# A linear-attention and gated-MLP mixer on one core: the query features of the first row pair are turned early and stored turned

## The chip, the cores and the metric

One core of one Trainium2 chip runs the kernel. The metric is the device time of one execution in microseconds (us); of several runs the median is given. The engines are TensorE (PE), VectorE (DVE), ScalarE (ACT), GpSimd (POOL) and SyncE (SP); SP and POOL also issue DMA transfers.

## What is computed

x has 2048 rows of 512 values, in float32. After a layernorm two branches are added to it:

```python
xn = layernorm(x)
q, k, v = heads(xn @ wqkv)                 # 32 heads of 16
phi(t) = [softmax(t @ w_phi), softmax(-t @ w_phi)]     # 32 features a head
o = phi(q) (phi(k)^T v) / (phi(q) . sum(phi(k)) + 1e-6)
z = gelu(xn @ w_in); z1, z2 = z[:, :688], layernorm(z[:, 688:])
g = w_sp @ z2 + b_sp                       # w_sp is 2048 x 2048
out = x + o @ wo + (z1 * g) @ w_out
```

## The kernel before

The rows are 16 tiles of 128 (NT), or 8 pairs (NP). Every large product is made of three TensorE passes over float32 operands that are split in a high and a low half: L56 high by high, L57 high by low, L58 low by high (function mm3). ScalarE rounds the high half (L48, names in h), VectorE subtracts to get the low one (L52, names in l).

The stages follow one another, and TensorE has work in each:

- *Projections.* q, k, v and z1. The features of q, unnormalised, go to DRAM (e_d, one 128x1088 block a tile, with the inverse sums), z1 to z_d.
- *The z1 tail* (L631 to L647): the last z1 rows; zb, the sum of phi(k) over all rows, and kvT; then for the tiles s = 0 and 1 the features are loaded back (load_q) and normalised on VectorE (q_fin, L542 to L549: a multiplication with zb, a reduction, small steps, a reciprocal, a multiplication). The finished tile is stored to e_d by SP (L647). That store, `early`, is what the 15 copies of x into out (`seeds`, L708) are issued after, and behind them on SP stand 11 loads of w_sp (wf, L568).
- *The z2 stage* (L704 on): z2 of all tiles, gelu on ScalarE, layernorm statistics on VectorE (BN_STATS, L719), and b_split, which writes the B operands of the next stage.
- *The g stage* (products n = 0 to NC-1): w_sp times z2 by a seven-product scheme, four quarters a pair of row tiles; `drain` collects the products in c (L771 to L776), `gate` multiplies with z1, and `turn` transposes the gated pair in blocks of 32x32 on VectorE (L795, z1t<-c) and stores it to u_d with four DMAs (L798), for pair NP-2 = 6 through POOL and for the others through SP. In its last quarters the loads of the last stage are started too: zb, u of tiles 0 and 1, and with first_q the normalised features of tiles 0 and 1 (eq<-e_d, L835).
- *The last stage* (L993 on). For each pair of tiles: `attend_T` turns the features on TensorE (16 transposes, ptq, L934/L936) and ScalarE copies the four results to SBUF (f, L938); `project_u` is the product with w_out (pout, 15 matmuls by mm3 and two of L965), whose operands uh and ul are split from u; `attend` is the product with kvT (po, L951) and its split in oT high (ACT) and oT low (DVE); `project_o` adds oT times wo into pout; ScalarE copies pout and POOL adds it into out (L983, L984). Before the first pair the wo loads (16 DMAs, L808) are issued and split in woh and wol. Between the pairs VectorE normalises the features of the tiles three ahead (`features`), and POOL copies them (er<-et, L905) to the buffer that the transposes read.

Which instruction follows which on an engine is set by the Tile scheduler when the program is built, from its own estimate of the times; `tc.issue_after` lays down that an instruction may not be placed before another one. Each engine then works its list in order, and an instruction that waits holds up all behind it. Buffers come from pools; a tile placed where an earlier tile was waits for the last use of that one, a DMA's end too. The stage pool of the attention (cwk) lies where the buffers of the g stage were.

Of the kernel before, what the change touches and what calls it, by code (L numbers as in the profile page):

```python
# [10 lines left out]
F32 = mybir.dt.float32  # L11
F32R = mybir.dt.float32r
# [6 lines left out]
P = 128  # L19
# [4 lines left out]
NG = 4  # L24
NF = 2 * D
# [3 lines left out]
BL = 32  # L29
# [4 lines left out]
NP = NT // 2  # L34
# [6 lines left out]
def mixer(ctx: ExitStack, tc: tile.TileContext, x, x_t, wv, wqkT, phi_bd, wo, w_in, wst, b_r, w_out, out):  # L41
    nc = tc.nc
    pe, act, dve, pool, sp = nc.tensor, nc.scalar, nc.vector, nc.gpsimd, nc.sync
# [20 lines left out]
    left = lambda name, bufs: pool_of(name, bufs, side="left")  # L64
# [10 lines left out]
    dram = ctx.enter_context(tc.tile_pool(name="dram", bufs=1, space=DRAM))  # L75
    e_d = dram.tile([NT, P, NF + 2 * H], F32, name="e_d")
    z1_d = dram.tile([NT, P, FH], F32, name="z1_d")
    u_d = dram.tile([NT, FU, P], F32, name="u_d")
    kvT_d = dram.tile([P, D], F32, name="kvT_d")
    zb_d = dram.tile([P, NF], F32, name="zb_d")  # L80
    nm_d = dram.tile([NT, ND, P], F32, name="nm_d")

    ident = cst.tile([P, P], F32, name="ident")
# [16 lines left out]
    def group(e, j):  # L100

        return e[:, j * P:(j + 1) * P]
# [72 lines left out]
    with ExitStack() as p0:  # L175
# [236 lines left out]
        t = xz_tile(2 * D, F32R, "xT").rearrange("p (a b) -> p a b", a=2)  # L412
# [18 lines left out]
        p = ps.tile([P, D], F32, tag="mm", name="proj")  # L431
# [7 lines left out]
        p = ps.tile([P, D], F32, tag="mm", name="proj")  # L439
# [18 lines left out]
        p = ps.tile([P, D], F32, tag="mm", name="proj")  # L458
# [79 lines left out]
    def q_fin(et, tmp, zb):  # L538

        e, r, t, w = et[:, :NF], *(et[:, NF + k * 2 * H:NF + (k + 1) * 2 * H] for k in range(3))  # L540
        den = et[:, NF + 6 * H:QW]
        dve.tensor_tensor(tmp, e, zb, op=ALU.mult)  # L542
        dve.tensor_reduce(t, heads(tmp), axis=AX.X, op=ALU.add)
        dve.tensor_tensor(t, t, r, op=ALU.mult)
        dve.scalar_tensor_tensor(den, pairs(t, 0), EPS_DEN, pairs(t, 1), op0=ALU.add, op1=ALU.add)
        dve.reciprocal(den, den)
        dve.tensor_tensor(w.rearrange("p (h a) -> p h a", a=2), r.rearrange("p (h a) -> p h a", a=2),
                          den.unsqueeze(2).to_broadcast([P, H, 2]), op=ALU.mult)
        return e, dve.tensor_tensor(heads(e), heads(e), bc(w, 2 * H), op=ALU.mult).ins  # L549

    QC = 4
    NQ = NT // QC
    NC = NP * NQ
# [43 lines left out]
    NE = 2  # L597
    with ExitStack() as p1:
        tmp1 = p1.enter_context(left("tmp1", 1))
        kvT = tmp1.tile([P, D], F32, name="kvT")  # L600
        zb = tmp1.tile([P, NF], F32, name="zb")
        zhl = tmp1.tile([P, 4, D], F32R, tag="zhl", name="zhl")
        psk = p1.enter_context(psum("psk", 2))

        def make_zb():

            ones_r = tmp1.tile([P, P], F32R, name="ones_r")
            round_h(act, ones_r, ones)
            for k in range(2):
                pz = psk.tile([P, D], F32, tag="kvt", name="pz")  # L610
                cs = slice(k * D, (k + 1) * D)
                h, l = (zhl[:, 2 * k + n] for n in range(2))
                round_h(act, h, zacc[:, cs])
                rest_l(l, zacc[:, cs], h)
                pe.matmul(pz, ones_r, h, start=True, stop=False)
                pe.matmul(pz, ones_r, l, start=False, stop=True)
                dve.tensor_copy(zb[:, cs], pz)

        def make_kvT():
            kvm = zw.tile([P, 4, FC], F32, tag="T", name="kvm").rearrange("p a b -> p (a b)")[:, :D]  # L620
            kvm = kvm.rearrange("p (g b) -> p g b", b=P)
            dve.tensor_tensor(kvm.rearrange("p g (k b) -> p g k b", k=2),
                              kv_acc.unsqueeze(2).to_broadcast([P, NG, 2, HP]),
                              mask.rearrange("p (k b) -> p k b", k=2).unsqueeze(1).to_broadcast([P, NG, 2, HP]),
                              op=ALU.mult)
            pt = psk.tile([P, NG, P], F32, tag="kvt", name="kvt")
            for g in range(NG):
                pe.transpose(pt[:, g], kvm[:, g], ident)
            act.activation(kvT, pt.rearrange("p g b -> p (g b)"), AF.Copy)

        for j in range(2):  # L631
            load_win(w2[j], 2 + j)
        for s in range(NT - LAG, NT):
            z1_raw(tmp1, (za, zbp)[s % 2], s, 2)
            if s == NT - LAG + 1:
                make_zb()
        make_kvT()
        raw[0], raw[1] = load_a(0), load_a(1)
        A[0] = prep_a(0, raw.pop(0))
        sp.dma_start(kvT_d, kvT)  # L640
        sp.dma_start(zb_d, zb)
        tb = p1.enter_context(left("tmp1b", 1))
        for s in range(NE):
            et = load_q(s, tb.tile([P, QW], F32, name="et") if s else tmp1.tile([P, 4, D], F32, tag="zhl", name="et").rearrange("p a b -> p (a b)")[:, :QW])
            tmp = zw.tile([P, 4, FC], F32, tag="z2", bufs=2, name="qtmp").rearrange("p a b -> p (a b)")[:, :NF]
            e, _ = q_fin(et, tmp, zb)
            early = sp.dma_start(e_d[s, :, :NF], e).ins  # L647
    ctx_w1.__exit__(None, None, None)
    ctx_zc = psum("zc", 1)
    zc = ctx_zc.__enter__()  # L650
# [53 lines left out]
    for s in range(NT):  # L704
        p = zproj((kv_ps_p, zc, zbp, za)[s % 4], s, w2, (0, 1) if s % 2 == 0 else (1, 0))
# [7 lines left out]
        for k, q in p:  # L713
            ins = act.activation(z[:, k], q, AF.Gelu_apprx_tanh, scale=r_x[:, s:s + 1]).ins
# [87 lines left out]
    def slot(name, dt=F32):  # L802
        return xz_tile(2 * FH, dt, name)
# [26 lines left out]

    lasts, wu = [None] * 9, []

    def first_q(s):
        e = slot("eq", F32R)[:, :NF]
        sp.dma_start(e.bitcast(F32), e_d[s, :, :NF])  # L835
        return e

    def stage_w():
        t = [xz2.tile([P, SL], F32, tag="b", name="wof") for _ in range(3)]
        w = [xz_tile(2 * D, F32R, "wu") for _ in range(KF + 1)]  # L840
# [7 lines left out]
    g, es, ets = {}, {}, {}  # L848
    for n in range(NC):
        i = SEQ[n][0]  # L850
        if n % NQ == 1 and i < NP - 1:
            z = load_z1(i)
        products(n, g)
        if n % NQ == NQ - 1 and i < NP - 1:
            c = gt.tile([P, 2, FU], F32, tag="c", name="c")
            cq = c[:, :, :FH].rearrange("p k (j f) -> p k j f", j=2)
            cb = drain(i, g, cq)
            g = {}
        if n + 3 < NC:
            raw[n + 3] = load_a(n + 3)  # L860
        if n + 2 < NC:
            A[n + 2] = prep_a(n + 2, raw.pop(n + 2))
        if n % NQ == NQ - 1 and i < NP - 1:
            turn = gate(i, cb, z, c, z, prep_a.last)
            if i < NP - 2:
                turn()
        if n == NC - 4:
            stage_w()
        if n == NC - 3:
            zs = slot("zb", F32R)  # L870
            zb, ident_r = zs[:, :NF].bitcast(F32), zs[:, NF:NF + P]
            round_h(act, ident_r, ident)
            sp.dma_start(zb, zb_d)
            uT = [first_gate(0)]
            ets[2] = load_q(2, slot("et"))
            es[2], last = q_fin(ets.pop(2), slot("qtmp")[:, :NF], zb)
        if n == NC - 2:
            es[0], es[1] = first_q(0), first_q(1)
            t = xz_tile((KF + 1) * P, F32R, "u1")
            us = {1: load_u(1, k_tiles(t[:, :KF * P]).bitcast(F32), t[:2 * REM, KF * P:(KF + 1) * P])}  # L880
    cb = drain(NP - 1, g, slot("c").rearrange("p (k j f) -> p k j f", k=2, j=2))
# [9 lines left out]
    fin = []  # L891
# [33 lines left out]
    def attend_T(s):  # L925

        fs = []
        for g in range(NG):
            pt = pst.tile([P, 2, 2, P], F32, tag="tr", name="ptq")
            for a in range(2):  # L930
                for k in range(2):
                    src = group(es[s + k], 2 * g + a)
                    if src.dtype == F32:
                        pe.transpose(pt[:, a, k], src, ident)  # L934
                    else:
                        pe.transpose(pt[:, a, k].bitcast(F32R), src, ident_r)  # L936
            f = wk.tile([P, 2, 2 * P], F32, tag="f", bufs=NG + 1, name="f")
            lasts[5] = act.activation(f, pt.rearrange("p a k b -> p a (k b)"), AF.Copy).ins  # L938
            fs.append(f)
        return fs  # L940
# [49 lines left out]

    GATE_LAST = 8

    fT = attend_T(0)  # L993
    wk.tile([P, D], F32, tag="xr", bufs=3, name="xr")
    wk.tile([P, 10 * QP], F32, tag="gap", name="gap")
    wk.tile([P, NG, 2 * P], F32R, tag="oTh", name="oT")
    with tc.issue_after(lasts[5]), tc.issue_after(lasts[1]), tc.issue_after(fin[-1]):
        for c in range(ND):
            rows = [(m * QP, (m + 1) * QP) for m in range(c // 2 * 8 + c % 2, (c // 2 + 1) * 8, 2)]
            load_w(wo, rows, wo_h[:, c], wo_l[:, c], cw.tile([P, D], F32, tag="wof", bufs=4, name="wof"))  # L1000
# [15 lines left out]
    p, nxt = {}, dict(enumerate(uT))  # L1016
    for i in range(0, NT, 2):
# [24 lines left out]
        if i + 2 < NT:  # L1042
            with tc.issue_after(lasts[4]):
                fT = attend_T(i + 2)
# [33 lines left out]
```

## Time and profile before

| | us |
|---|---|
| median of 3 runs | 625.21 |
| the runs | 624.02, 625.21, 629.76 |
| the profiled execution, its own time | 625.34 |
| span of its trace | 623.6 |
| granted TensorE clock | 0.999 |

The stages in this execution: the z1 tail ends and the z2 stage runs to 278, the g stage from 278 to 490, the last stage from 490 to the end. The profile gives start and duration of each instruction; `x12` behind a row means twelve instructions in a row that are shown as one, and a bracket names the idle time of the engine ahead of it and what ended it. Matmuls are pipelined, so that their durations overlap and the distance of two starts is what one costs. SPq and POOL rows named DMA_DIRECT2D are issues of transfers; when the data landed stands in the view of a line ("DMA to landing").

### The profile page before, as it was taken

To read this page: it belongs to the slowest core of one execution; us is meant where nothing else is said; L and a number is where in the kernel's file an instruction comes from. 1 tells how busy PE (TensorE), PEld (TensorE's weight loads), DVE (VectorE), ACT (ScalarE), POOL (GpSimd) and SP (SyncE) were. 2 spreads that over 40 slices of the span, in tenths; PEclk is the share of its full clock that TensorE was granted. 3 is DMA by queue.
4 is the path that set the end of the run, shared out by engine and by line. 5 is a ranking of instruction groups with operands and counts; after the bars stand their busy time and mean duration, and the time that the engine had idled before them with its cause. 6 is when DMAs were issued, how large, how long until landed. Compare 5 with 4: busy or idle time off the path is not lost.

```text
span 623.6 us, 11439 instructions
## 1 busy us (share of the span) xinstructions
PE 615.1 (99%) x4366; PEld 561.5 (90%) x4366; DVE 508.3 (82%) x903; ACT 272.8 (44%) x436; POOL 113.7 (18%) x198
## 2 busy tenths in 40 slices
PE   8999999999999999999999999999999999999997
PEld 7888888878889999999999999999999887788785
DVE  5999899899988498988989888696959899989211
ACT  4652324333433558876435433253444433334331
POOL 4122233222211025541000000000000212211110
PEclk9999999999999999999999999999999999999999
DMA  9557676566546757002464745637477799984722
GB/s 318 189 138 165 162 183 187 152 165 172 118 154 186 271 210 270 2 1 67 129 128 136 196 89 155 156 97 173 88 177 244 225 284 332 328 243 111 162 38 48
DMA packets 90671, 103.67 MB, mean 166 GB/s; under 512 B 47080, under 2 KB 60136, under 8 KB 90376
## 3 DMA queue, kind: packets, MB, share of 16 engines
q1 hardware_dynamic: 76840, 60.76, 34.0%
q0 software_dynamic: 11472, 36.54, 23.6%
q10 hardware_dynamic: 2304, 5.64, 2.4%
q8 instruction: 34, 0.56, 0.4%
q14 instruction: 21, 0.17, 0.1%
HBM read 61.61 MB, written 30.56 MB: 148 GB/s over the span
## 4 chain that ended last, share of the span: by engine, by line
PE 85%; DMA 6%; DVE 4%; issue 3%; POOL 1%; ACT 1%; DVEq 0%; POOLq 0%
PE g L58 11%; PE g L57 10%; PE g L56 10%; PE zps L58 6%; PE zps L56 6%; PE zps L57 6%; PE pout L56 5%; PE pout L58 5%; PE pout L57 5%; DMA xc<-nm_d 5%; PE proj L56 4%; PE proj L57 4%; PE proj L58 4%; PE ptq L936 1%; PE po L951 1%
## 5 line engine op out<-in xcount | busy, mean ns | idle before, releaser
L57 PE MATMUL g<-B,A 128*128 128x344 f32 x448 | 143.4, 320 | 0.0
L56 PE MATMUL g<-B,A 128*128 128x344 f32 x448 | 142.9, 320 | 0.0
L58 PE MATMUL g<-B,A 128*128 128x344 f32 x448 | 140.7, 321 | 0.1
L56 PEld LDWEIGHTS g<-B,A 128*128 128x128 f32 x448 | 84.3, 188 | 0.0
L57 PEld LDWEIGHTS g<-B,A 128*128 128x128 f32 x448 | 84.2, 188 | 0.0
L58 PEld LDWEIGHTS g<-B,A 128*128 128x128 f32 x448 | 83.7, 188 | 0.4 <-DVE A L52 0.4
L48 ACT ACTIVATE A<-S 128x512 fp32r<-128x512 f32 x64 | 39.2, 629 | 76.3 <-DVE S L588 61.3
L121 ACT ACTIVATE e<-e,r_x 128x1024 f32<-128x1024 f32 x26 | 29.9, 1150 | 56.3 <-DVE e L120 55.1
L56 PE MATMUL proj<-wqk_h,xT 128*128 128x512 f32 x128 | 50.1, 391 | 0.0
L57 PE MATMUL proj<-wqk_l,xT 128*128 128x512 f32 x128 | 50.0, 390 | 0.0
L58 PE MATMUL proj<-wqk_h,xT 128*128 128x512 f32 x128 | 49.9, 390 | 0.0
L48 ACT ACTIVATE A<-wf 128x512 fp32r<-128x512 f32 (+1 forms) x64 | 33.1, 519 | 33.3 <-DMA wf<-in_wst 12.6
L52 DVE TENSOR_TENSOR A<-S,A 128x512 fp32r<-128x512 f32 x64 | 43.0, 686 | 4.4 <-ACT A L48 4.0
L56 PE MATMUL zps<-w_0h,xT 128*128 128x344 f32 x128 | 41.1, 321 | 0.0
L56 PE MATMUL zps<-w_1h,xT 128*128 128x344 f32 x128 | 40.9, 319 | 0.0
L58 PE MATMUL zps<-w_0h,xT 128*128 128x344 f32 x128 | 40.8, 319 | 0.0
L58 PE MATMUL zps<-w_1h,xT 128*128 128x344 f32 x128 | 40.7, 319 | 0.0
L57 PE MATMUL zps<-w_1l,xT 128*128 128x344 f32 x128 | 40.6, 318 | 0.0
L57 PE MATMUL zps<-w_0l,xT 128*128 128x344 f32 x128 | 40.6, 318 | 0.0
L753 POOL DMA_DIRECT2D z1t<-z_d x16 | 8.6, 545 | 166.9 <-DMA u_d<-z1t 124.9
L52 DVE TENSOR_TENSOR A<-wf,A 128x512 fp32r<-128x512 f32 (+1 forms) x64 | 35.0, 549 | 1.8 <-ACT A L48 1.8
L124 DVE TENSOR_REDUCE sm<-e 128x64 f32<-128x1024 f32 x26 | 31.2, 1200 | 1.7 <-ACT e L121 1.5
(218 smaller groups left out, 1430.6 us busy)
## 6 DMA issues: line engine op xcount, KB each, us to landing
wf<-in_wst SPq DMA_DIRECT2D x64, 256.0 KB, 3.1
e_d<-e POOLq DMA_DIRECT2D x16, 544.0 KB, 5.0
et<-e_d SPq DMA_DIRECT2D x16, 544.0 KB, 5.2
er<-et POOLq DMA_DIRECT2D x12, 512.0 KB, 5.5
z_d<-z1f ACTq DMA_DIRECT2D x16, 344.0 KB, 2.3
z1t<-z_d POOLq DMA_DIRECT2D x16, 344.0 KB, 5.3
zacc<-e POOLq DMA_DIRECT2D x10, 512.0 KB, 4.7
u<-u_d SPq DMA_DIRECT2D x15, 320.0 KB, 6.3
```

The source lines that it names most:

```text
L48: return act.activation(h, src, AF.Copy).ins
L52: return (eng or dve).tensor_tensor(l, src, h.bitcast(F32), op=ALU.subtract).ins
L56: pe.matmul(dst, ah, bh, start=start, stop=False)
L57: pe.matmul(dst, ah, bl, start=False, stop=False)
L58: return pe.matmul(dst, al, bh, start=False, stop=stop).ins
L121: softmax_pair.last = less, act.activation(e, e, AF.Exp, scale=scale).ins
L124: dve.tensor_reduce(sm, heads(e), axis=AX.X, op=ALU.add)
L753: pool.dma_start(t[:, k, :FH], z1_d[2 * i + k])
L936: pe.transpose(pt[:, a, k].bitcast(F32R), src, ident_r)
L951: lasts[3] = pe.matmul(po[r][c * QP:(c + 1) * QP, k], kvT[rows, m // 2, cols], fs[m // 4][rows, m // 2 % 2], start=True, stop=True).ins
```

## The change

The two tiles that are finished in the z1 tail are no longer stored to e_d as they are. VectorE transposes each in blocks of 32x32 (turn_q), tile 0 into the memory of zb, tile 1 into that of tile 0's features, and four SP DMAs a tile store the blocks, in runs of 128 bytes, to a new DRAM tensor q_d, which holds the features of the pair turned. In the g stage, where eq was loaded, four SP loads bring the turned features as f tiles (128x2x256 in two buffers, the form that attend_T gives). The call attend_T(0) is gone, and the wo loads are no longer placed behind its last copy (lasts[5]). The other seven pairs are treated as before.

```diff
--- before.py
+++ after.py
@@ -78,6 +78,7 @@
     u_d = dram.tile([NT, FU, P], F32, name="u_d")
     kvT_d = dram.tile([P, D], F32, name="kvT_d")
     zb_d = dram.tile([P, NF], F32, name="zb_d")
+    q_d = dram.tile([NP, NF, 2, P], F32, name="q_d")
     nm_d = dram.tile([NT, ND, P], F32, name="nm_d")
 
     ident = cst.tile([P, P], F32, name="ident")
@@ -548,6 +549,18 @@
                           den.unsqueeze(2).to_broadcast([P, H, 2]), op=ALU.mult)
         return e, dve.tensor_tensor(heads(e), heads(e), bc(w, 2 * H), op=ALU.mult).ins
 
+    def turn_q(s, dst, e):
+
+        ins = dve.transpose(dst, e).ins
+        q = q_d[s // 2, :, s % 2].rearrange("(m j) t -> j m t", j=BL)
+        for b in range(0, P, BL):
+            turn_q.last = sp.dma_start(q[:, :, b:b + BL], dst[b:b + BL].rearrange("p (m t) -> p m t", t=BL)).ins
+        return ins
+
+    def load_f(s, f, g):
+        sp.dma_start(f, q_d[s // 2, 2 * g * P:2 * (g + 1) * P].rearrange("(a p) k t -> p a (k t)", p=P))
+        return f
+
     QC = 4
     NQ = NT // QC
     NC = NP * NQ
@@ -639,12 +652,14 @@
         A[0] = prep_a(0, raw.pop(0))
         sp.dma_start(kvT_d, kvT)
         sp.dma_start(zb_d, zb)
-        tb = p1.enter_context(left("tmp1b", 1))
+        tb, done = p1.enter_context(left("tmp1b", 1)), []
         for s in range(NE):
             et = load_q(s, tb.tile([P, QW], F32, name="et") if s else tmp1.tile([P, 4, D], F32, tag="zhl", name="et").rearrange("p a b -> p (a b)")[:, :QW])
             tmp = zw.tile([P, 4, FC], F32, tag="z2", bufs=2, name="qtmp").rearrange("p a b -> p (a b)")[:, :NF]
-            e, _ = q_fin(et, tmp, zb)
-            early = sp.dma_start(e_d[s, :, :NF], e).ins
+            done.append(q_fin(et, tmp, zb)[0])
+        for s in range(NE):
+            turn_q(s, done[s - 1] if s else zb, done[s])
+        early = turn_q.last
     ctx_w1.__exit__(None, None, None)
     ctx_zc = psum("zc", 1)
     zc = ctx_zc.__enter__()
@@ -830,11 +845,6 @@
 
     lasts, wu = [None] * 9, []
 
-    def first_q(s):
-        e = slot("eq", F32R)[:, :NF]
-        sp.dma_start(e.bitcast(F32), e_d[s, :, :NF])
-        return e
-
     def stage_w():
         t = [xz2.tile([P, SL], F32, tag="b", name="wof") for _ in range(3)]
         w = [xz_tile(2 * D, F32R, "wu") for _ in range(KF + 1)]
@@ -875,7 +885,10 @@
             ets[2] = load_q(2, slot("et"))
             es[2], last = q_fin(ets.pop(2), slot("qtmp")[:, :NF], zb)
         if n == NC - 2:
-            es[0], es[1] = first_q(0), first_q(1)
+            fT = []
+            for k in range(0, NG, 2):
+                t = slot("f")[:, :NF].rearrange("p (g a t) -> p g a t", g=2, a=2)
+                fT += [load_f(0, t[:, j], k + j) for j in range(2)]
             t = xz_tile((KF + 1) * P, F32R, "u1")
             us = {1: load_u(1, k_tiles(t[:, :KF * P]).bitcast(F32), t[:2 * REM, KF * P:(KF + 1) * P])}
     cb = drain(NP - 1, g, slot("c").rearrange("p (k j f) -> p k j f", k=2, j=2))
@@ -990,11 +1003,10 @@
 
     GATE_LAST = 8
 
-    fT = attend_T(0)
     wk.tile([P, D], F32, tag="xr", bufs=3, name="xr")
     wk.tile([P, 10 * QP], F32, tag="gap", name="gap")
     wk.tile([P, NG, 2 * P], F32R, tag="oTh", name="oT")
-    with tc.issue_after(lasts[5]), tc.issue_after(lasts[1]), tc.issue_after(fin[-1]):
+    with tc.issue_after(lasts[1]), tc.issue_after(fin[-1]):
         for c in range(ND):
             rows = [(m * QP, (m + 1) * QP) for m in range(c // 2 * 8 + c % 2, (c // 2 + 1) * 8, 2)]
             load_w(wo, rows, wo_h[:, c], wo_l[:, c], cw.tile([P, D], F32, tag="wof", bufs=4, name="wof"))
```

The program's lists change with it: TensorE has 16 transposes fewer, ScalarE four copies fewer, VectorE two transpositions more, SP eight stores for two and four loads for two. Lines below the change are 10 to 15 lines further down (L936 is L949, L771 is L786, L549 is L550).

On ScalarE at the entry of the last stage; before (c is the last drain, uh<-u_5457 belongs to tile 1, oT to the first pair):

```order
L772 ACTIVATE c<-g 128x344
L48 ACTIVATE uh<-u_5457 128x640
L938 ACTIVATE f<-ptq 128x512 x4
L48 ACTIVATE woh<-wof 128x512 x4
L48 ACTIVATE oT<-po 128x2x256 x2
L48 ACTIVATE uh<-u 128x640 x2
```

and now:

```order
L787 ACTIVATE c<-g 128x344
L48 ACTIVATE woh<-wof 128x512 x4
L48 ACTIVATE uh<-u_5468 128x640
L48 ACTIVATE oT<-po 128x2x256 x2
L48 ACTIVATE uh<-u 128x640 x2
```

The copies f are gone, and uh of tile 1 has moved behind the four woh.

On VectorE at the same place, with the semaphores that each row waits for (DMAHW are transfers that SP issued, DMASW transfers of POOL); before:

```order
L795 STREAM_TRANSPOSE z1t<-c 128x1472
L52 TENSOR_TENSOR ul<-u_5457,uh 128x640 [waits DMAHW0_49,Activation_49]
L52 TENSOR_TENSOR wol<-wof,woh 128x512 [waits DMAHW5_49,DMAHW4_49,DMAHW6_49,DMAHW3_49,Activation_49]
L52 TENSOR_TENSOR wol<-wof,woh 128x512 [waits DMAHW2_49,DMAHW1_49,DMAHW7_49,DMAHW0_49,Activation_49]
L52 TENSOR_TENSOR wol<-wof,woh 128x512 [waits DMAHW5_49,DMAHW4_49,DMAHW6_49,DMAHW3_49,Activation_49]
L52 TENSOR_TENSOR wol<-wof,woh 128x512 [waits DMAHW2_49,DMAHW1_49,DMAHW7_49,DMAHW0_49,Activation_49]
L52 TENSOR_TENSOR oT<-po,oT 128x2x256 [waits Activation_49] x2
L542 TENSOR_TENSOR qtmp<-et,zb 128x1024 [waits DMAHW3_49]
```

and now:

```order
L810 STREAM_TRANSPOSE z1t<-c 128x1472
L52 TENSOR_TENSOR ul<-u_5468,uh 128x640 [waits DMAHW0_49,Activation_49]
L52 TENSOR_TENSOR wol<-wof,woh 128x512 [waits DMAHW5_49,DMAHW6_49,DMAHW4_49,DMAHW3_49]
L52 TENSOR_TENSOR wol<-wof,woh 128x512 [waits DMAHW2_49,DMAHW7_49,DMAHW1_49,DMAHW0_49]
L52 TENSOR_TENSOR wol<-wof,woh 128x512 [waits DMAHW5_49,DMAHW6_49,DMAHW4_49,DMAHW3_49]
L52 TENSOR_TENSOR wol<-wof,woh 128x512 [waits DMAHW2_49,DMAHW7_49,DMAHW1_49,DMAHW0_49]
L52 TENSOR_TENSOR oT<-po,oT 128x2x256 [waits DMASW1_49,DMASW2_49,DMASW0_49,DMASW3_49,DVE_49,Activation_49]
L52 TENSOR_TENSOR oT<-po,oT 128x2x256 [waits Activation_49]
L543 TENSOR_TENSOR qtmp<-et,zb 128x1024 [waits DMAHW3_49]
```

The order is the same; the first low half of oT has four waits for POOL's transfers more. These four are the stores u_d<-z1t of pair 6, and the DVE wait is for the transposition in the first row. In SBUF that oT tile lies from byte 199072 of each partition on, where it lay from 209312 on before, and z1t of pair 6 takes the bytes 195040 to 200928: the f tiles (5 buffers of 2048 bytes) were the first allocation of the pool, ahead of oT, and now come behind it.

On VectorE one pair later, in the features of tile 5 (the second of the third pair); before, with the low halves of oT at the second pair after the last step (L549) of tile 5:

```order
L546 RECIPROCAL et<-et 128x32
L52 TENSOR_TENSOR ul<-u,uh 128x640
L547 TENSOR_TENSOR et<-et 128x64
L549 TENSOR_TENSOR et<-et 128x1024
L542 TENSOR_TENSOR qtmp<-et,zb 128x1024
L52 TENSOR_TENSOR oT<-po,oT 128x2x256 x2
```

and now:

```order
L545 TENSOR_TENSOR et<-et 128x64
L546 SCALAR_TENSOR_TENSOR et<-et 128x32
L547 RECIPROCAL et<-et 128x32
L52 TENSOR_TENSOR oT<-po,oT 128x2x256
L548 TENSOR_TENSOR et<-et 128x64
L52 TENSOR_TENSOR oT<-po,oT 128x2x256
L550 TENSOR_TENSOR et<-et 128x1024
```

The low halves of oT now stand ahead of the last step of tile 5, L550, which POOL's copy er waits for.

## The prediction

> **What bounds the kernel now.** I read the page first, its busy times, slices and chain:
>
> ```profile
> PE 615.1 (99%) x4366; PEld 561.5 (90%) x4366; DVE 508.3 (82%) x903; ACT 272.8 (44%) x436; POOL 113.7 (18%) x198
> DVE 5999899899988498988989888696959899989211
> PE 85%; DMA 6%; DVE 4%; issue 3%; POOL 1%; ACT 1%; DVEq 0%; POOLq 0%
> ```
>
> TensorE is busy for 99% of the span and makes 85% of the chain. An edit pays only by taking TensorE work away, and costs only where it makes TensorE wait. So next comes TensorE's timeline where the edit removes work, the passage from the last g product to the last stage, and the transposes of the third and fourth pair:
>
> ```profile
> 490.01 0.32 PE L58 MATMUL g<-B,A 128*128 128x344 f32 x1
> 491.39 1.23 PE L936 MATMUL ptq<-zb,eq 128*128 128x128 f32 x12 [0.77 <-DVE c L771]
> 492.46 0.46 PE L56 MATMUL pout<-wu,u_uh 128*128 128x512 f32 x1
> ...
> 496.52 1.09 PE L951 MATMUL po<-f,kvT 64*32 64x256 f32 x32
> 497.55 0.50 PE L56 MATMUL pout<-wu,uh 128*128 128x512 f32 x1
> ...
> 502.48 0.39 PE L58 MATMUL pout<-woh,oT 128*128 128x512 f32 x1
> ...
> 523.28 1.47 PE L936 MATMUL ptq<-zb,er 128*128 128x128 f32 x16
> ...
> 539.18 1.50 PE L936 MATMUL ptq<-zb,er 128*128 128x128 f32 x16
> ```
>
> Sixteen transposes (four of them ahead of this row) and a wait of 0.77 stand between the last g (490.01 to 490.33) and the first pout (492.46): about 2.1 us that the edit can give back at most. From 492.46 to 540 no row of this timeline has an idle time, so every other engine is just in time or early. How early decides what a shift costs; hence the rows of ScalarE, of VectorE, and of the queues of SyncE and GpSimd in this stretch:
>
> ```profile
> 486.79 0.74 ACT L48 ACTIVATE uh<-u 128x640 fp32r<-128x640 f32 x1 [1.66 <-DMA u<-u_d]
> ...
> 495.66 0.63 ACT L48 ACTIVATE woh<-wof 128x512 fp32r<-128x512 f32 x1 [0.56 <-DMA wof<-in_wo]
> ```
>
> ```profile
> 489.73 0.52 DVE L776 TENSOR_TENSOR c<-g,c 128x344 f32<-128x344 f32 x1
> ...
> 493.36 0.79 DVE L52 TENSOR_TENSOR ul<-u,uh 128x640 fp32r<-128x640 f32 x1
> 494.10 1.90 DVE L52 TENSOR_TENSOR wol<-wof,woh 128x512 fp32r<-128x512 f32 x3
> 496.32 0.69 DVE L52 TENSOR_TENSOR wol<-wof,woh 128x512 fp32r<-128x512 f32 x1 [0.33 <-ACT woh L48]
> 498.34 1.29 DVE L52 TENSOR_TENSOR oT<-po,oT 128x512 fp32r<-128x512 f32 x2 [1.32 <-ACT oT L48]
> 499.54 1.22 DVE L542 TENSOR_TENSOR qtmp<-et,zb 128x1024 f32<-128x1024 f32 x1
> ...
> 514.45 1.23 DVE L549 TENSOR_TENSOR et<-et 128x1024 f32<-128x1024 f32 x1
> ...
> 525.70 1.23 DVE L549 TENSOR_TENSOR et<-et 128x1024 f32<-128x1024 f32 x1
> ```
>
> ```profile
> 483.82 8.44 SPq L808 DMA_DIRECT2D wof<-in_wo  x16
> ```
>
> **The change, part by part.**
>
> (1) *The transposes of the first pair go.* The first pout then waits for its PSUM only (the c row, done at 490.25) and starts near 490.35: 2.1 us earlier. Sixteen matmul rows and four copies of f are gone.
>
> (2) *ScalarE's order.* In the built program the four woh copies now stand ahead of the copy uh of the second row tile, which before was done at 487.53. The fourth woh needs the last of 16 wo loads and started at 495.66, after a wait for that load. SyncE issues two loads more ahead of these (four f for two eq), so I take 495.7 to 496.0: woh ends at 496.3 to 496.6, uh (0.74) at 497.1 to 497.4. TensorE's first pout took 492.46 to 496.52, 4.06 us, and po 1.03. In the changed kernel they end at 490.35 + 5.09 = 495.4, and TensorE stands until 497.1 to 497.4, where it was at 497.55 before. Of the 2.1 us some 0.3 is left. VectorE is worse off: ul waits for uh, and the four wol stand behind ul. From 497.1, with 0.79 + 1.90 + 0.69, they end at 500.5 where they ended at 497.0.
>
> (3) *A new wait.* In the built program the first low half of oT (the VectorE row of 498.34) has four waits more: for GpSimd's four stores of z1t, the turned gate of pair 6. The reason is placement: the five f tiles (10,240 bytes a partition) are no longer the first that this pool takes, so that oT's low half moves from byte 209312 to 199072, into 195040 to 200928 where z1t lies. These stores are late, as GpSimd's timeline shows; the second row is the view of line 798 cut to the last of the four, issued at 496.8:
>
> ```profile
> 494.06 3.63 POOL L798 DMA_DIRECT2D u_d<-z1t  x4 [36.90 <-ACT woh L48]
> ```
>
> ```profile
> DMA to landing us min/median/max: 9.0/9.0/9.0
> ```
>
> 496.8 + 9.0 = 505.8. The transposition that feeds the stores has the same place behind the same c rows, and the same loads (u, rt, et, wo) compete with them, so I keep this landing. The first half of the VectorE pair takes 0.65: TensorE's first L58 product of oT starts at 506.5 and not at 502.48. That is **+4.05**, and it swallows parts 1 and 2: TensorE merely idles elsewhere.
>
> (4) *What is queued behind it.* VectorE waits in order, so qtmp of tile 3, at 499.54 before, comes at 507.1: 7.5 us late, while TensorE is 4.05 late. VectorE cannot catch up, for it is busy for 4.86 of these 5 us, and the DMA engines are full (share 0.98):
>
> ```profile
> 500.00:505.00 5.00, 5.00 (x24) 4.09 (x22) 4.86 (x9) 0.77 (x2) 0.00 (x0) 1.00 0.98 293
> ```
>
> Who needs it: the copy er of tile 5, a GpSimd transfer behind the multiplication at 514.45, and behind er the transposes at 523.28. Its issue in GpSimd's timeline, and the view of line 905 cut to it:
>
> ```profile
> 516.25 0.54 POOL L905 DMA_DIRECT2D er<-et  x1 [4.76 <-issue]
> ```
>
> ```profile
> DMA to landing us min/median/max: 6.5/6.5/6.5
> ```
>
> It landed at 522.75, 0.5 before its use. In the new order the low halves of the second pair's oT (1.29) also stand before that multiplication, so er is issued at 516.25 + 7.5 + 1.2 = 525.0 and lands at 531.5. TensorE is at 523.28 + 4.05 = 527.3, does the four transposes of tile 4's copy (0.4) and stands until 531.5: **+3.7**. With a landing of 5.5 it is 2.7, with 8.0 it is 5.2. Tile 7's copy is in time: its multiplication, at 525.70 to 526.9 before, ends 7.5 later at 534.4, and even with a landing of 9.0 er is there at 544, while its transposes (539.18) come at 546.9. VectorE is nearly idle in the last three slices, so its lateness costs nothing more, and a TensorE that is busy to the end gives nothing back.
>
> (5) *The turn itself, in the z2 stage.* Two transpositions of 128x1024, priced from the group of the first row, 1704 / 1472 x 1024 = 1185 ns each, 2.4 us in all, and eight stores of 128 KB for two of 512 KB. Below it stand the sum of the windows from 230 to 279 and SyncE's rows:
>
> ```profile
> L795 DVE STREAM_TRANSPOSE z1t<-c 128x1472 f32<-128x1472 f32 x7 | 11.9, 1704 | 0.0
> ```
>
> ```profile
> sum 49.00, PE 49.00 PEld 49.00 DVE 41.98 ACT 39.47 POOL 22.82; mean PE 9.80 PEld 9.80 DVE 8.40 ACT 7.89 POOL 4.57
> ```
>
> ```profile
> 232.83 10.76 SPq L708 DMA_DIRECT2D out<-in_x  x15
> 284.59 2.79 SPq L568 DMA_DIRECT2D wf<-in_wst  x2
> ```
>
> TensorE has no idle time in these 49 us and VectorE has 7.0, more than the 2.4; SyncE has nothing to issue from 243.6 to 284.6. I take 0; without this cover it is 2.4. The q_d stores are issued at about 0.95 each (GpSimd's 3.63 for four), to 240. What may wait for them is the B operands that are next written over the memory they read; that is a bound for the last rival. The f loads stand where the eq loads stood, ahead of the wo loads from 483.82 on; with the 9.0 of the slowest store they are there by 493, and po comes at 494.4: hidden.
>
> *The sum*: 4.05 + 3.7 = 7.75, against the profiled execution's 625.34 (span 623.6). I take off 0.2, as TensorE may do a few products of the next tile while it waits. The median of the runs, 625.21, is 0.13 lower: 625.21 + 7.55 = **632.8**.
>
> **The rivals.**
>
> - *The z1t stores land early.* All stores of line 798 have these landings:
>
> ```profile
> DMA to landing us min/median/max: 4.4/5.0/9.0
> ```
>
> With the median the last lands at 501.8, the low half is done at 502.5, and the first wait shrinks to some 0.3. VectorE is then 3.5 late because of part 2, er goes out at 521.0 and lands at 527.5 against 523.3 + 0.3 + 0.4: +3.5 more. Time 629.0. Against it: the four went 5.5 to 9.0 one after another, in a stretch where the DMA engines were full (0.98 in the row above).
>
>   [...]
> - *Only the first wait counts.* If er lands in some 3 to 4 us, TensorE hardly waits again: +4.4, 629.6. For it: er is alone on its queue then; against it: the landing of 6.5 that I read.
> - *The other side: the DMA engines are less loaded from 490 to 500.* If the last wo load lands by 494.0 and not 495.6, uh is ready when po ends at 495.4, and if the z1t stores also land by 500, the 2.1 us stay: 623.1. It decides at 1.6 us less for wo. Nothing lightens that stretch: the bytes are the same.
> - *The turn is not covered.* Its 2.4 comes on top: 635.2. VectorE's 7.0 us of idle time are spread over the stage, so a part could show; and a q_d store that lands late could hold the B operands for as long.
>
>   [...]
>
> **How the numbers follow.** Forecast 0.57, early landing 0.14, first wait only 0.12, other side 0.05, turn not covered 0.12. The two cases below the forecast hold 0.26 and lie at 629.0 and 629.6; the case above is at 635.2. The range 627.8 to 635.2 takes these in and leaves out the other side and the tails, some 0.15. A measurement of this kernel can tell about 1%, 6.25 us, from no change. Slower by more (over 631.5): nine tenths of 0.57 and of 0.12, 0.62. Faster by more would need 6.25 us where 2.1 are at stake: 0.02. Within 1%: 0.36.
>
> **What would show it.** TensorE: pout directly behind g near 490.4; idle before the second pout on ACT uh, about 1.7 to 2; before an L58 product of oT, about 4 to 4.5, on VectorE's oT; before ptq<-zb,er, about 3.7, on the GpSimd transfer er. VectorE: idle near 500.5 to 505.8 ahead of oT. The z2 stage as long as before. Wrong, if oT's low half starts before 502, if er's transposes have no idle time, or if the first g product comes later than 278.

## The result and the profile after

The changed kernel takes 633.18 us (median of 10 runs, 628.84 to 636.55) against 625.93 (10 runs, 624.02 to 629.76). The ratio is 1.0112, with a 95% interval of 1.0085 to 1.0139: about 7 us slower. The profiled execution has a span of 631.7 against 623.6.

The page of the changed kernel, in its busy times, granted clock and chain:

```profile
PE 616.9 (98%) x4350; PEld 560.6 (89%) x4350; DVE 509.7 (81%) x905; ACT 268.7 (43%) x432; POOL 113.7 (18%) x198
...
PEclk9999999999999999999999999999999979999999
...
PE 58%; DMA 14%; DVE 12%; issue 7%; POOL 5%; ACT 3%; SPq 1%; POOLq 0%; DVEq 0%; ACTq 0%
```

TensorE executes 16 instructions fewer and is busy for 1.8 us more, and one slice has a clock below 9 tenths. Both point to one place. TensorE's timeline there, from the last g product to the transposes of the third pair:

```profile
491.51 0.32 PE L58 MATMUL g<-B,A 128*128 128x344 f32 x1
492.11 0.47 PE L56 MATMUL pout<-wu,u_uh 128*128 128x512 f32 x1 [0.27 <-DVE c L791]
...
496.19 1.09 PE L964 MATMUL po<-f,kvT 64*32 64x256 f32 x32
497.55 0.50 PE L56 MATMUL pout<-wu,uh 128*128 128x512 f32 x1 [0.26 <-ACT uh L48]
...
508.51 0.80 PE L58 MATMUL pout<-woh,oT 128*128 128x512 f32 x1 [5.69 <-DVE oT L52]
509.11 0.63 PE L56 MATMUL pout<-woh,oT 128*128 128x512 f32 x1
...
512.39 0.39 PE L58 MATMUL pout<-woh,oT 128*128 128x512 f32 x1
...
531.22 1.47 PE L949 MATMUL ptq<-zb,er 128*128 128x128 f32 x16
```

The last product starts at 626.68, where it started at 618.74 before: 7.94 us later. The rows divide this. From the last g product to the first L58 product of oT it is 17.00 us (508.51 - 491.51) where it was 12.47: +4.53. From there to the third pair's transposes it is 22.71 where it was 20.80: +1.91. Of this 1.81 lies in the first nine steps: from 508.51 to the row of 512.39 it is 3.88, and before, from 502.48 to this row, 2.07:

```profile
504.55 0.61 PE L58 MATMUL pout<-woh,oT 128*128 128x512 f32 x2
```

From the third pair's transposes on it is 95.46 in both. What is left, 1.50, was lost before 491.51: the g stage begins at 278.35 (277.98 before) and its first and last product are 213.16 apart (212.03 before).

What TensorE waits for at 508.51 stands in VectorE's timeline, and behind that are GpSimd's stores, with their landings:

```profile
498.27 2.49 DVE L52 TENSOR_TENSOR wol<-wof,woh 128x512 fp32r<-128x512 f32 x4
507.77 1.29 DVE L52 TENSOR_TENSOR oT<-po,oT 128x512 fp32r<-128x512 f32 x2 [7.00 <-DMA u_d<-z1t]
```

```profile
495.78 3.64 POOL L813 DMA_DIRECT2D u_d<-z1t  x4 [35.94 <-DVE z1t L810]
```

```profile
DMA to landing us min/median/max: 6.6/7.0/9.1
```

VectorE stands for 7.0 us before oT's low half until z1t is stored: the last of the four stores goes out at 498.5 and lands 9.1 later.

### The profile page after: what moved, and what is told of

It is laid out like the page before. It is cut to its first block, busy times and chain, and to the rows that moved or that the text cites. A ratio compares the mean times of both kernels' runs of the same rounds, so it can differ in the third digit from the quotient of the medians.

```text
span 631.7 us, 11412 instructions
## 1 busy us (share of the span) xinstructions
PE 616.9 (98%) x4350; PEld 560.6 (89%) x4350; DVE 509.7 (81%) x905; ACT 268.7 (43%) x432; POOL 113.7 (18%) x198
## 4 chain that ended last, share of the span: by engine, by line
PE 58%; DMA 14%; DVE 12%; issue 7%; POOL 5%; ACT 3%; SPq 1%; POOLq 0%; DVEq 0%; ACTq 0%
PE g L56 7%; PE g L58 7%; PE g L57 7%; PE pout L56 5%; PE pout L58 5%; PE pout L57 5%; PE proj L57 4%; PE proj L56 4%; PE proj L58 4%; DMA xc<-nm_d 4%; DMA wf<-in_wst 3%; DMA u_d<-z1t 2%; POOL rstd L96 2%; PE zps L57 1%; PE zps L58 1%
## 5 line engine op out<-in xcount | busy, mean ns | idle before, releaser
L58 PE MATMUL g<-B,A 128*128 128x344 f32 x448 | 140.4, 321 | 0.0
L58 PEld LDWEIGHTS g<-B,A 128*128 128x128 f32 x448 | 83.6, 188 | 0.1
L58 PE MATMUL proj<-wqk_h,xT 128*128 128x512 f32 x128 | 49.9, 390 | 0.0
L58 PE MATMUL zps<-w_0h,xT 128*128 128x344 f32 x128 | 40.8, 319 | 0.0
L58 PE MATMUL zps<-w_1h,xT 128*128 128x344 f32 x128 | 40.7, 319 | 0.0
```

The source lines that it names most:

```text
L58: return pe.matmul(dst, al, bh, start=False, stop=stop).ins
```

## The experiments

Each row gives the ratio to the kernel before, measured beside it on the same chip (runs 1 to 4, 5 to 7, 8 to 10 and the repeat of 7 were on four chips), and from one profiled execution the span of the g stage (first to last g product) and of the last stage (last g product to the last product of all).

| kernel | ratio (95%) | g stage | last stage |
|---|---|---|---|
| before | 1 | 212.03 | 128.73 |
| the change | 1.0112 (1.0085 to 1.0139) | 213.16 | 135.17 |
| 1: change, f first | 1.0024 (1.001 to 1.0038) | 212.96 | 128.67 |
| 2: and uh ahead of woh | 1.0016 (0.9996 to 1.0035) | 213.95 | 128.25 |
| 3: before, oT over z1t | 1.0094 (1.0074 to 1.0115) | 212.02 | 132.81 |
| 4: change, wait filled with matmuls | 1.0152 (1.0127 to 1.0177) | 212.63 | 137.92 |
| 5: as 2, without the transpositions | 1.0016 (0.9997 to 1.0034) | 212.03 | 128.46 |
| 6: as 3, wait filled in part | 1.0120 (1.0098 to 1.0142) | 212.05 | 136.45 |
| 7: as 2, tile 5 not copied | 0.9987 (0.9974 to 1.0000) | 212.52 | 126.43 |
| 7 once more | 0.9981 (0.9970 to 0.9992) | 213.98 | 126.41 |
| 8: change, tile 5 not copied | 1.0109 (1.0094 to 1.0123) | 212.51 | 134.91 |
| 9: as 1, tile 5 not copied | 1.0003 (0.9994 to 1.0013) | 212.82 | 127.85 |
| 10: before, tile 5 not copied | 1.0001 (0.9984 to 1.0018) | 212.05 | 127.75 |

One execution's spans are not the kernel's own to the last tenth. The two profiles of run 7 differ by 1.46 in the g stage. And the last stage of before holds the wait of 0.77 us for c that the prediction shows ahead of the first pair's transposes; runs 3 and 10, with the same instructions there, have no such wait, and run 6 has 0.24.

### Is it the placement, or the order? (1, 2, 3)

Run 1 takes an f tile from the pool ahead of oT, so that oT's low half lies where it lay before. It waits for no store then, and ScalarE's entry to the last stage is in the order of the change.

```diff
     GATE_LAST = 8
 
+    wk.tile([P, 2, 2 * P], F32, tag="f", bufs=NG + 1, name="f")
     wk.tile([P, D], F32, tag="xr", bufs=3, name="xr")
```

> The change, with one tile of the f buffers taken from the pool first, so that oT's low half lies where it lay before and waits for no store; every engine's order stays that of the change. Theory (placement): TensorE's wait of 5.7 us ahead of the L58 product of oT is gone, and with it the half clock of 506 to 512. The entry is 1.5 us ahead of before at the second pout and the z2 and g stages 1.5 us behind, so the time comes out near 626, ratio 1.000 (0.997 to 1.003). Rival (order): the copy uh behind the four woh makes VectorE late, and the copy er of tile 5 stalls TensorE by about 3 us: near 629, ratio 1.005.

Measured 627.04, ratio 1.0024. The wait is gone and some four fifths of the loss with it; the rival's 629 (ratio 1.005) lies outside the interval, and so does the theory's 1.000 (its range reached to 1.003). TensorE's waits in the last stage are these two:

```profile
498.13 0.50 PE L56 MATMUL pout<-wu,uh 128*128 128x512 f32 x1 [1.07 <-ACT uh L48]
...
525.21 1.23 PE L949 MATMUL ptq<-zb,er 128*128 128x128 f32 x12 [0.63 <-DMA er<-et]
```

They are the uh of part 2 and the copy of tile 5 of part 4, each at a smaller size, and the copy without the store that part 4 held for the cause. The last stage is as long as before: what the transposes and the wait ahead of them took has been given back, 1.70 us of it in these two waits.

Run 2 also puts uh ahead of woh:

```diff
-    with tc.issue_after(lasts[1]), tc.issue_after(fin[-1]):
+    with tc.issue_after(lasts[0]), tc.issue_after(lasts[1]), tc.issue_after(fin[-1]):
```

> As the run before, and the copy uh of tile 1 stands ahead of the four woh again, as before the change. Theory (placement): 0.3 us less than the run before it, since the second pout waited 0.26 us for uh: 625.5, ratio 0.999. Rival (order): 2 to 3 us less than the run before it, as VectorE's ul and wol come 3 us sooner.

Measured 627.08, ratio 1.0016: against run 1 no difference that can be told. The profile shows why. The wait for uh is gone, and the next one has grown:

```profile
525.72 1.23 PE L949 MATMUL ptq<-zb,er 128*128 128x128 f32 x12 [1.31 <-DMA er<-et]
```

Run 3 is the converse: the kernel before, with nothing turned early, and only oT taken from the pool ahead of f.

```diff
-    fT = attend_T(0)
     wk.tile([P, D], F32, tag="xr", bufs=3, name="xr")
     wk.tile([P, 10 * QP], F32, tag="gap", name="gap")
     wk.tile([P, NG, 2 * P], F32R, tag="oTh", name="oT")
+    wk.tile([P, NG, 2 * P], F32R, tag="oTl", name="oT")
+    fT = attend_T(0)
```

> The kernel before, with oT taken from the pool ahead of f, so that oT's low half lies over z1t as in the change; nothing else is moved, no feature is turned early. Theory (placement): the low half waits for the last z1t store at 505.8, the L58 product moves from 502.5 to 506.5, +4.0, and TensorE's clock is halved for some 6 us after the wait, +1.9: 631.8, ratio 1.0095. Without the clock's part 629.9, ratio 1.0065. Rival (order): unchanged, ratio 1.000.

Measured 631.47, ratio 1.0094, as expected with the clock's part, though the profiled execution divides it otherwise (below). So the placement alone, without the change, costs most of what the change costs. TensorE's timeline and its clock (second number from the right of each window is the DMA share, the third the clock):

```profile
503.81 0.50 PE L58 MATMUL pout<-woh,oT 128*128 128x512 f32 x1 [2.62 <-DVE oT L52]
504.14 0.59 PE L56 MATMUL pout<-woh,oT 128*128 128x512 f32 x1
504.53 0.63 PE L57 MATMUL pout<-wol,oT 128*128 128x512 f32 x1
```

```profile
502.00:504.00 2.00, 0.19 (x1) 0.19 (x2) 0.94 (x2) 0.74 (x1) 0.00 (x0) 1.00 0.95 325
504.00:506.00 2.00, 2.00 (x6) 1.57 (x6) 2.00 (x3) 0.00 (x0) 0.00 (x0) 0.54 1.19 307
506.00:508.00 2.00, 2.00 (x7) 1.55 (x6) 1.90 (x5) 0.01 (x1) 0.00 (x0) 0.61 1.03 281
```

Here the stores landed within 7.5 us, the wait was 2.62, and the clock still fell to half. In this profile the L58 product comes 14.30 us after the last g product (+1.83; the wait of 2.62, less about the 0.77 for c that before has there), and what follows it takes 2.25 us more than before; the timed runs, with 5.8 us, lost more than the profiled one, in which the last stage is 4.08 longer.

### Does the half clock cost? (4, 6)

Run 4 puts 24 matmuls on TensorE into the wait of the change; they write a tile that nobody reads.

```diff
+                if i == 0 and c == 0:
+                    pe.matmul(q, oT[0][:, c, ts], wo_h[:, c, cs], start=False, stop=False)
+                    last = pe.matmul(q, oT[0][:, c, ts], wo_l[:, c, cs], start=False, stop=False).ins
+                    spin = pst.tile([P, D], F32, tag="tr", name="spin")
+                    for n in range(24):
+                        with tc.issue_after(last):
+                            last = pe.matmul(spin, oT[0][:, c, ts], wo_h[:, c, cs], start=n == 0, stop=n == 23).ins
```

> The change, with 24 matmuls of 128x512 added on TensorE right ahead of the L58 product that waits for oT's low half; they write a PSUM tile that nobody reads and take 24 x 0.229 = 5.5 us of the 5.7 us wait. Theory (clock): the wait is not idle any more, the granted clock stays at 1.0, the products behind it take 0.39 and not 0.63 us, and the time falls by 1.9 to 631.3, ratio 1.008. Rival (late copies): the 1.9 us between the wait and the transposes of the third pair come from VectorE's or GpSimd's lateness, and the time stays at 633.2, ratio 1.011, or rises by what the matmuls overrun.

Measured 635.48, ratio 1.0152. Half of the theory held: the clock stayed at 1.0 in this whole stretch, and the products behind the wait took 0.39 us. The time did not fall:

```profile
501.68 5.63 PE L999 MATMUL spin<-woh,oT 128*128 128x512 f32 x24
507.71 0.50 PE L1001 MATMUL pout<-woh,oT 128*128 128x512 f32 x1 [0.40 <-DVE oT L52]
...
514.30 1.86 PE L947 MATMUL ptq<-ident,et 128*128 128x128 f32 x15 [1.42 <-DVE et L550]
528.27 0.50 PE L58 MATMUL pout<-woh,oT 128*128 128x512 f32 x1 [2.15 <-DVE oT L52]
```

TensorE at full speed ran into VectorE, which was late since it had waited for the same stores: 1.42 + 2.15 us. In the change no such wait shows. That its slow clock covers them is argued and not shown, for the added matmuls also changed the scheduler's order (the second pair's transposes are no longer split around 12 products, and oT's low half stands behind tile 5's features); so the run doesn't say what full speed in the change's own order would give.

Run 6 fills the shorter wait of run 3 with eight such matmuls, with TensorE's order kept; VectorE's order changes behind the wait.

```diff
-                    for n in range(24):
+                    for n in range(8):
```

> The kernel before with the shifted oT, and 8 matmuls of 128x512 into an unread PSUM tile in the place of the wait (8 x 0.229 = 1.8 us of the 3 us); TensorE's list is otherwise the same. Theory (clock): the idle time left is about 1.2 us, the clock stays at 1.0, and of the 5.8 us that the shift cost 1.9 come back: 629.6, ratio 1.006. Rival (lateness): what the halved clock took is taken by VectorE's lateness instead, in waits for et or oT, and the ratio stays near 1.009.

Measured 632.92, ratio 1.0120: worse, and inconclusive. The stores landed later than in run 3 (up to 9.5 us, not 7.5), so that 3.11 us of idle time were left behind the eight matmuls, and the clock halved all the same (0.50 from 506 to 508). Later TensorE waited for the second pair's oT too, as the rival says, for 1.31 us (0.27 in run 3):

```profile
506.00 0.80 PE L988 MATMUL pout<-woh,oT 128*128 128x512 f32 x1 [3.11 <-DVE oT L52]
...
525.70 0.50 PE L58 MATMUL pout<-woh,oT 128*128 128x512 f32 x1 [1.31 <-DVE oT L52]
```

Whether the half clock costs anything beyond the lateness that it covers stays open.

### Step 4, and where the removed work goes (7 to 10)

Run 8 is the change, with tile 5 left out of GpSimd's copies; TensorE transposes it from et.

```diff
-        if s == 3:
+        if s in (3, 5):
             return
```

> The change, with tile 5 transposed straight from et, so that GpSimd's copy er of tile 5 is no longer in TensorE's way; oT's low half still lies over z1t. Step 4 of the prediction (the late copy of tile 5 costs 3.7 us): 3.5 us less than the change, near 629.6, ratio 1.006. Rival (the profile of the change: er was there in time, and the loss is the wait for z1t and the slow clock behind it): no change against the change, ratio 1.011.

Measured 633.34, ratio 1.0109: no change against the change. The 3.7 us of part 4 (step 4) are refuted: in the change nothing waited for that copy.

Run 7 makes the same edit in run 2.

> The run with f first and uh ahead of woh, and tile 5 isn't copied by GpSimd: TensorE transposes it from et as it does tile 3. Theory (late copy): the 1.3 us that TensorE waited for er go, against 0.2 us for eight slower transposes: 1.0 us less than that run, 626.0, ratio 1.0000 (0.998 to 1.002). Rival: VectorE itself is what is late, and the wait moves to et or to oT's low half: no change, 1.0016.

Measured 624.69, ratio 0.9987, better than expected; the last stage is 126.43 us, 2.30 shorter than before. Its interval touches 1, so it ran again:

> The same kernel as the run that gave 0.9987 (0.9974 to 1.0000), once more, since that interval just touches 1. If the gain of the turned features is real (2.3 us less in the last stage, 0.5 us more in the g stage), the ratio is 0.996 to 0.999 again; if it was chance, 1.000 and above.

Measured 624.85, ratio 0.9981 (0.9970 to 0.9992). This version beats both kernels, by 0.1 to 0.2%.

Run 9 puts uh behind woh again:

> The run that gave 0.9987 (f first, uh ahead of woh, tile 5 from et) with uh behind the four woh again, as in the change. Theory (once nothing else is late, the order of uh counts): TensorE waits about 1.1 us for uh at the second pout, as in the run with f first alone; ratio 1.0005. Rival (TensorE gets this time back, as between the first two runs, which came out equal): 0.9987.

Measured 626.29, ratio 1.0003. Once nothing else is late, the order of one ScalarE copy costs its full wait, 1.17 us at the second pout.

Run 10 is the control, the kernel before with tile 5 from et:

> The kernel before, with tile 5 transposed straight from et and nothing else. Control for the run that gave 0.9987. Theory (the gain there comes from the turned features; before, TensorE did not wait for tile 5's copy): eight transposes in float32 cost some 0.2 us, ratio 1.0003. Rival (the gain comes from leaving out the copy): 0.998 to 0.9987.

Measured 626.09, ratio 1.0001: leaving out the copy by itself gives nothing that can be told. Its interval (0.9984 to 1.0018) still holds 0.9987, so the times alone don't exclude the rival. The profiles do: from the first L58 product of oT to the last product of all it is 116.25 here and 116.26 before, and what run 7 gains lies ahead of that. These are the rows behind the last g product, first in run 10 (last g at 491.16), then in run 7 (490.54):

```profile
491.32 1.50 PE L936 MATMUL ptq<-zb,eq 128*128 128x128 f32 x16
492.65 0.47 PE L56 MATMUL pout<-wu,u_uh 128*128 128x512 f32 x1
```

```profile
490.70 0.43 PE L56 MATMUL pout<-wu,u_uh 128*128 128x512 f32 x1
```

The first pout comes 1.49 us after the last g in run 10 and 0.16 in run 7. So the transposes are worth 1.33 us; the rest of the 2.1 was the wait for c, which doesn't come in every execution. Against run 10 the last stage of run 7 is 1.32 shorter.

### What makes the g stage longer? (5)

Run 5 is run 2 without the two transpositions; the first pair's features are stored in a wrong order and its attention is computed from them.

```diff
-        ins = dve.transpose(dst, e).ins
+        dst, ins = e, None
```

> The run with f first and uh ahead of woh, less the two transpositions of VectorE: the features are stored to q_d as they are, so that the first pair's attention is computed from features in a wrong order. All engines' lists up to the last stage are then those of before (SP's eight stores aside). Theory (schedule): the 1 us that the g stage takes longer in the change comes from the order in which the scheduler put VectorE's and ScalarE's work after it had fitted in the two transpositions; without them the g stage lasts 212.0 again, the start of g is at 278.0, and the time is 625.3, ratio 0.999 (0.9975 to 1.0005). Rival (stores): the eight stores in 128-byte runs do it; then the g stage lasts 213 as before and the ratio stays 1.0016.

Measured 626.79, ratio 1.0016. The span of the g stage agrees with the theory: 212.03, with the same eight stores. All five profiles of kernels without the transpositions (before is one) have 212.02 to 212.05, all eight with them (the change, and run 7 twice) 212.51 to 213.98. That excludes the stores. The transpositions lie at 230 to 235 in the change and the two waits below at 294 and 336, which points to the new order that came with them, and not to their own 2.4 us. The waits of TensorE in the g stage of the change, 0.7 us, account for most of its 1.1:

```profile
PE g L56 <- DVE c L791: 0.4, 1, 0.4
PE g L56 <- ACT A L48: 0.3, 1, 0.3
```

The time came out at 1.0016 and not at 0.999 (the interval, 0.9997 to 1.0034, still holds a part of the range expected). The profile can't settle it: its g stage begins at 280.40 and not at 278.0, and 2.2 us of that were lost in the first stage, long before anything that is edited (the first product into zps starts at 27.52, and at 25.35 before). In the last stage TensorE lost what it had gained, as VectorE and the copy er were late:

```profile
508.61 1.53 PE L947 MATMUL ptq<-ident,et 128*128 128x128 f32 x12 [0.92 <-DVE et L550]
...
525.69 1.24 PE L949 MATMUL ptq<-zb,er 128*128 128x128 f32 x12 [0.73 <-DMA er<-et]
```

## Why the prediction came out right, and where its steps were wrong

Forecast 632.8, measured 633.18. That the number fits is luck. Half of the forecast, 3.7 us, was for a wait that did not come; 3.41 came from two places that the sum put at nothing, 1.91 behind the first wait and 1.50 ahead of the last g product. The main term, the wait for z1t, was right.

- *Part 1, the transposes gone.* As forecast: pout follows 0.60 us behind the last g product (0.35 forecast, 0.27 of it a wait for c), not 2.45.
- *Part 2, the order of uh.* Right in kind, too large here. The second pout waited 0.26 us for uh and not 1.7 to 2: the g stage ended 1.5 later, the fourth woh only 0.58 later (496.24), so that ScalarE was nearly in time. Runs 8, 1, 4 and 9, with the same order, show the wait at 0.41, 1.07, 1.08 and 1.17.
- *Part 3, the new wait.* Right: place, cause and landing (9.1 us against 9.0). It cost 4.53 against the 4.05 of the sum. The stores went out 1.72 later, but 1.50 of that is the later end of the g stage; the difference is made up of 0.2 from the stores, 0.1 from the landing, and 0.2 from the landing to the product (507.6 to 508.51, 0.9 where 0.7 was forecast). Runs 1 and 3 show the cause from both sides. The lower end of the range, 627.8, lies 2.5 above the profiled 625.34; no run shows a term of this size for early stores: in the kernel before the four took 5.5 to 9.0 us to land, and in run 3, where they landed earliest (the slowest in 7.5), the wait still came and the median rose by 5.8.
- *Part 4, "what is queued behind it".* This step failed. VectorE was late as forecast: er of tile 5 went out at 526.68, 35.2 us behind the last g product, where the forecast has 35.0 (525.0 - 490.01). But it landed in 3.1 us, not in 6.5, before TensorE came:

```profile
526.68 0.54 POOL L918 DMA_DIRECT2D er<-et  x1 [5.71 <-PE pout L978]
```

```profile
DMA to landing us min/median/max: 3.1/3.1/3.1
```

The step that was wrong is the landing, taken from one row of before. It is what decided: by 6.5 er would have been there at 533.2, and TensorE, which began the third pair at 531.22, would have waited some 1.6 us even with the slow clock; by 3.1 it was there at 529.8, about when TensorE would have wanted it even 1.81 us earlier (an estimate: 531.22 - 1.81 and 0.4 for tile 4's transposes). Over the twelve er copies of each of six profiles (before, the change, runs 1 to 4) this landing ranges from 2.9 us (run 4) to 9.4 (before). In the change the DMA engines had less to do where er was issued, a share of 0.65 in that window (first) against 1.06 in the kernel before (second); that this shortened it fits, but no run tries it.

```profile
526.00:528.00 2.00, 2.00 (x10) 1.65 (x9) 2.00 (x4) 0.00 (x0) 0.54 (x1) 1.00 0.65 252
```

```profile
516.00:518.00 2.00, 2.00 (x10) 1.66 (x9) 2.00 (x4) 0.70 (x1) 0.54 (x1) 1.00 1.06 373
```

For er this is the rival "only the first wait counts", to which the prediction gave 0.12; its time, 629.6, did not come, because of the terms that the sum lacked. One of the prediction's signs of being wrong, "if er's transposes have no idle time", came true.
- *The term that the sum lacked.* The clock, in windows of the changed kernel:

```profile
504.00:506.00 2.00, 0.00 (x0) 0.00 (x0) 0.00 (x0) 0.00 (x0) 0.00 (x0) 0.85 1.04 289
506.00:508.00 2.00, 0.00 (x0) 0.00 (x0) 0.23 (x1) 0.00 (x0) 0.00 (x0) 0.50 1.05 337
508.00:510.00 2.00, 1.49 (x4) 1.20 (x5) 2.00 (x3) 0.00 (x0) 0.00 (x0) 0.50 0.31 105
510.00:512.00 2.00, 2.00 (x6) 1.61 (x5) 2.00 (x4) 0.00 (x0) 0.00 (x0) 0.50 0.00 1
512.00:514.00 2.00, 2.00 (x9) 1.57 (x9) 1.86 (x7) 0.48 (x1) 0.00 (x0) 0.94 0.60 170
```

It falls at about 505.4 (0.85 in the first window) and is at half until about 512.2, although TensorE works again from 508.51 on. The products take 0.63 and start 0.43 apart, not 0.23: seven steps from 509.11 to 512.10 take 2.99 us where 1.60 would do. That is 1.39 of the 1.81 found above; the rest lies in the steps before and behind them (0.60 and 0.29 for 0.23). The clock was back 3.7 us after the restart. It had fallen some 2.6 us after the end of TensorE's last product (502.8, as the profile models it), and in run 3 it fell with an idle time of 2.62.
- *Part 5, the turn in the z2 stage.* Its cover held (TensorE has no wait from 230 to 279), and the stores to q_d were not late; their landings in the change:

```profile
DMA to landing us min/median/max: 3.3/3.4/3.4
```

But it was not free. The scheduler, given two transpositions more, laid the later work of VectorE and ScalarE in another order, and the g stage took 1.13 longer, as run 5 confirms (0.5 to 2.0 over the eight profiles). The other 0.37, by the start of g, is no larger than what this time differs by among kernels whose lists agree there (277.33 to 279.11 in those that are the kernel before up to the last stage). So the sign "if the first g product comes later than 278", which came true at 278.35, could tell nothing: a kernel without the change starts at 279.11.

The sum by the runs: 4.53 + 1.91 + 1.50 = 7.94, against 4.05 + 3.70 - 0.2 = 7.55. The 0.2 for products of the next tile did not show either: TensorE has no product in the 5.69 us of its wait.

## What to carry to other kernels

A call that is taken away also takes away an allocation: whatever comes after it in the pool moves, and may come to lie over a buffer whose last store is still under way. So read the list of waits of the built program and not the diff alone. Work taken off the engine that bounds the kernel pays only when all that feeds the next stage is early enough by as much; here it took three edits (placement, one copy's order, one transfer left out) before the removed work, 1.3 us of transposes and in some executions a wait of up to 0.8, came out as a median 0.9 and 1.3 us lower.

## What the runs showed of the hardware

- TensorE's clock halved with idle times of 2.62 us (run 3), 3.11 (run 6), 5.40 (run 8) and 5.69 (the change), and not with 2.15 and 1.42 (run 4) and 1.31 (runs 2 and 6). The fall came 2.6 us (the change) to 3.3 (run 8) after the modelled end of the last product, an estimate from the clock of the windows; in run 3, 3.0 us after it, TensorE had by then started again. With the half clock the products behind the wait started 0.43 us apart and not 0.23, for 3.1 us (run 6) to 4.7 (run 8) from the restart.
- Four stores of 184 KB in runs of 128 bytes, issued 0.9 us apart on GpSimd's queue beside SyncE's loads (DMA share 1.02 from 496 to 508 in the change), took 5.5 us (before) to 10.4 (runs 1 and 4) to land over the profiles of all kernels but run 5, and the slowest of the four 7.5 (run 3) to 10.4. Eight stores of 128 KB in the same runs of 128 bytes, on SyncE's queue in the z2 stage, landed in 3.3 to 3.4 us in the change; what makes the difference, the queue or the load, was not tried. In the five kernels where oT's low half lies over z1t, VectorE waited 6.7 us (run 8) to 9.0 (run 6) for the stores of the first kind. The change's runs spread over 7.7 us, those of before over 5.7; that this is why was not tried.
